# Block-sparse attention and a gated feed-forward layer on one core: another opening, and the last output tile in column halves

## The chip, the cores and the metric

The kernel runs on one core of a Trainium2 chip. The metric is the device time of one execution in microseconds (us). The five engines work from queues of their own: TensorE (PE: matmuls and transposes), VectorE (DVE), ScalarE (ACT), GpSimd (POOL) and SyncE (SP); SP, ACT and POOL also issue DMA transfers. An engine takes its instructions strictly in the order in which they were written for it; an instruction that waits for a semaphore holds all behind it. All times below are us.

## The reference

q, k and v have the shape (4 batches, 8 heads, 768 rows, 64). The rows form 24 blocks of 32. A query block sees its own key block and its two neighbours, the first and the last block, and three sampled blocks; the first and last query block see all. The result goes through RMS normalization and a gated feed-forward layer of width 1536.

```python
scores = scale * np.matmul(q, k.transpose(0, 1, 3, 2))
mask = np.abs(blk_i - blk_j) <= window          # window = 1
mask = mask | (blk_i == 0) | (blk_j == 0) | (blk_i == n_blocks - 1) | (blk_j == n_blocks - 1)
for qb in range(n_blocks):
    for kb in sampled_blocks[qb]:
        mask[qb * block:(qb + 1) * block, kb * block:(kb + 1) * block] = True
scores = np.where(mask, scores, -1000000000.0)
# softmax over the keys, then attn @ v; heads side by side give x of (3072, 512)
xn = x / np.sqrt(np.mean(x * x, axis=-1, keepdims=True) + 1e-06) * rms_g
out = (silu(xn @ w_gate) * (xn @ w_val)) @ w_out
```

## The kernel before

**Tiling.** The 3072 rows are worked through in 12 chunks of 256 query rows, three a batch. A chunk's attention has 12 tiles: 4 pairs of heads, and for each pair 3 pairs of 128-row key tiles. For a tile PE makes the scores (`scores`, L605: four products into a PSUM tile of two banks), ACT their exponential over 1024 columns (`exp_`, L624), DVE multiplies by a 0/1 mask tile (`mask_`, L631), and PE multiplies with V (`av`, L638). In chunk 0 there is no mask multiply. There PE adds a large negative number to the masked scores with a second product per score product (L619; `PEM`, L210, says for which chunks: chunk 0, and chunk 1 for the first `PM1` pairs, and PM1 is 0). So exponentials of chunk 0 can start before the mask tiles exist.

When a chunk's attention is done, DVE normalizes (`o_norm`), the squares are summed (`square`), POOL takes the power (`rstd`), DVE scales (`scale_x`), and the 256 x 512 result is transposed: on PE (`x_transposes`, L693, with a copy out of PSUM, `x_copy`), or for the chunks of `XDMA` (L721) by DMA transposes from SP's queue (`x_dma`). Then the feed-forward part follows: for each of 6 pairs of 128-column slices the gate product gp and the value product vp on PE (L839), tanh on ACT (L845), two DVE products (`ff_uu`, `ff_h`), and at last y, 12 products of 512 columns for each half chunk (`ff_y`, L862), which `ff_o` (L870) copies to SBUF and stores.

**Loads.** Two plain fp32 loads stand at the start: all of K of the first pair of heads (`kf`, L226, 384 KB, SP's queue) and the first two of the six column groups of Q of that pair (`qf`, L227, 128 KB, ACT's queue), and ACT casts them to bf16 (`cast_first`). The sampled blocks (`samp_i`, L232) follow on SP. POOL then issues loads that cast to bf16 on the way: Q of the other three pairs (q28), K of pair 1 (k23), K of pairs 2 and 3 (k48), then V in two halves, the rest of Q (qrest, needed from chunk 1 on), and the weights in halves (wg, wv) and whole (wo). Batches 1 to 3 are loaded as fp32 into one buffer in turn (K, then Q, then V; L258), cast by ACT or DVE in six steps (`cast_c`), and transposed by DMA.

**Mask.** tid holds, for block b and column, the column's distance from the start of block b. Two DVE instructions make the 0/1 indicator `Kind` from it (L317 and L319: distance at least 0, and at most 31). `block_mask` makes a 24 x 24 block matrix `Bm` from three small index tiles (`jb`, which POOL makes after its first load, L367 to L369), and `block_samples` (L343) adds the samples: one cast, three compare-and-max steps, one copy into a second half. PE multiplies R (two identities) with Kind (`key_rows`, L487) and Bm with Kind (`mask_query`, L497), copies bring both to SBUF as `KindG` and `NegQ`, and from these two PE makes the penalty in chunk 0 and the mask tiles `Mk` later (`mask_tile`, `mask_copy`).

**Order.** All steps except the first instructions are tasks of a planner (class `Plan`). It keeps a clock for each engine, estimates start and end of each task from a duration, the ends of its dependencies (a name with `>` ahead only orders; others wait for the result), free buffers (`acq`, `rel`), an estimated landing of each DMA (`dma`, `extra`) and an earliest time (`after`). It always emits the task with the smallest estimated start, plus `SOFT` times its priority (`PRIO` by class, with a `BOOST` for some). So the order of the instructions in every engine's queue is fixed before the run, by estimates. Score tiles have a gate: tile i is held back while i is more than `LEAD` tiles, plus `SPEED` times the share of feed-forward work that is done, ahead. Warm-up matmuls on zeros stand at PE's start (7, L302), and up to 40 fill gaps till 32 us in the planner's clock.

Of the kernel before, what the change touches and what calls it, by code (L numbers as in the profile page):

```python
# [8 lines left out]
FP32 = mybir.dt.float32  # L9
# [6 lines left out]
START = dict(DVE=3.4, POOL=1.7, ACT=2.5, PE=4.4)  # L16
DMA0 = 3.0
HOLD = 191057930523.28
SOFT = 0.0032
LEAD = 34  # L20
BOOST = {'first': 0.1, 'x': 0.15, 'w': -0.2}
SPEED = 0.91
PRIO = {'av': -5, 'c': 38, 'dt': 17, 'e': -23, 'g': -12, 'h': 1, 'm': 39, 'mk': 31, 'mq': -46, 'mqc': 32, 'mt': -5, 'on': 0, 'rs': 113, 's': -8, 'sc': 61, 'sq': -45, 't': 9, 'th': -85, 'uu': -15, 'v': -5, 'va': 6, 'x': -1, 'xc': -3, 'xd': -22, 'xt': 29, 'y': 2, 'yo': 5}
# [133 lines left out]
def kernel(  # L157
# [60 lines left out]
    QAT = (4.6, 20.0, 31.0)  # L218
# [5 lines left out]
    kf = raw.tile([P, 2, NC * D], FP32, name="kf")  # L224
    qf = raw.tile([P, 2, 2 * D], FP32, name="qf")
    nc.sync.dma_start(out=kf, in_=kv[0, :, 0:2, :])  # L226
    nc.scalar.dma_start(out=qf, in_=qv[0, :, 0:2, 0:2 * D])  # L227
# [4 lines left out]
    nc.sync.dma_start(out=samp_i[0:NB, :], in_=s64)  # L232

# [37 lines left out]

    tid = const.tile([32, S], I32, name="tid")
# [8 lines left out]
    jb = const.tile([32, 2 * 32 + 1], I32, name="jb")  # L281
    nhalf = const.tile([P, 2], FP32, name="nhalf")
    nc.vector.memset(nhalf, -0.5)
    ones = const.tile([P, 2], FP32, name="ones")
    nc.vector.memset(ones[:, 0:1], 1.0)
    nc.vector.memset(ones[:, 1:2], -16384.0)
    Bm = const.tile([32, P], BF16, name="Bm")
# [15 lines left out]
    for i in range(FILL):  # L303
# [12 lines left out]
    tif = const.tile([32, S], BF16, name="tif")  # L316
    nc.vector.tensor_scalar(  # L317
        out=tif, in0=tid, scalar1=0.0, scalar2=None, op0=ALU.is_ge)
    nc.vector.scalar_tensor_tensor(  # L319
        out=Kindf, in0=tid, scalar=31.5, in1=tif, op0=ALU.is_le, op1=ALU.mult)  # L320
    for lo in (0, 64):
        nc.vector.tensor_copy(out=R[:, lo:lo + 32], in_=ident[0:32, 0:32])
# [3 lines left out]
    samp_f = const.tile([32, NRND], FP32, name="samp_f")  # L326

    def block_mask():
# [7 lines left out]
            op0=ALU.is_equal, op1=ALU.max)  # L336
        nc.vector.tensor_scalar(
            out=Bm[:, 0:NB], in0=near[:, 0:NB], scalar1=1.0, scalar2=edge[:, 1:2],
            op0=ALU.is_le, op1=ALU.max)
        nc.vector.memset(Bm[:, 0:1], 1.0)  # L340
        nc.vector.memset(Bm[:, NB - 1:NB], 1.0)

    def block_samples():  # L343
        nc.vector.tensor_copy(out=samp_f[0:NB, :], in_=samp_i[0:NB, 0:2 * NRND:2])
# [622 lines left out]
```

## Time and profile before

| | us |
|---|---|
| median of 8 runs | 306.73 |
| lowest and highest | 304.64, 308.43 |
| the profiled execution, whole | 308.42 |
| its span, first to last instruction | 306.4 |
| PE busy | 293.5 |
| DVE busy | 246.8 |
| ACT busy | 220.0 |
| POOL busy | 33.5 |
| DMA: bytes over the span | 35.37 MB, mean 115 GB/s |

The profile is one execution. A row of it gives start, length, engine, source line, operation, output and inputs, and in brackets how long the engine was idle before and what released it. In rows of a window, the busy times of the engines follow the window's length. The chain of waits is the chain of work that ended last, followed back from the end. A group's row of DMA transfers gives the time from issue to landing. The profiled execution is close to the highest of the runs.

### The profile page before, as it was taken

What the parts mean: (1) busy time and instruction counts of PE and PEld (TensorE: products, weight loads), DVE (VectorE), ACT (ScalarE), POOL (GpSimd) and SP (SyncE); (2) the same over time, 40 slices, a digit from 0 to 9 for tenths busy, and PEclk for the clock granted to TensorE, in tenths of its full rate; (3) what the DMA queues carried; (4) which work ended last, traced back from release to release, by engine and by line L of the source; (5) the groups of instructions that cost most, each with busy time, mean ns of one, the idle gap of its engine ahead of it and who ended that gap; (6) DMA issues with size and microseconds to landing.
All of it is one profiled execution on the core that took longest, in us unless ns stands there. A gap on an engine that the chain in (4) does not pass through costs nothing.

```text
span 306.4 us, 8007 instructions
## 1 busy us (share of the span) xinstructions
PE 293.5 (96%) x3377; PEld 209.1 (68%) x3404; DVE 246.8 (81%) x491; ACT 220.0 (72%) x311; POOL 33.5 (11%) x53
## 2 busy tenths in 40 slices
PE   8998999999999999879999999999999999999995
PEld 2675777685776777647677857866857857859582
DVE  6349999985798999588988999997977959948370
ACT  4699989455789788649879979887776778664231
POOL 9410000102002002020002011210000000000000
PEclk9999999999999999979999999999999999999999
DMA  7999981847900729979304293943002003000101
GB/s 124 288 210 210 208 268 33 202 158 201 201 3 2 242 58 168 137 126 239 51 19 156 89 237 141 175 137 103 4 30 76 2 2 105 0 36 34 36 34 68
DMA packets 38839, 35.37 MB, mean 115 GB/s; under 512 B 26068, under 2 KB 32212, under 8 KB 38804
## 3 DMA queue, kind: packets, MB, share of 16 engines
q0 software_dynamic: 10128, 21.76, 30.3%
q1 hardware_dynamic: 28260, 12.85, 19.2%
q8 instruction: 26, 0.43, 0.6%
q10 hardware_dynamic: 416, 0.26, 0.3%
q14 instruction: 9, 0.07, 0.1%
HBM read 28.57 MB, written 6.29 MB: 114 GB/s over the span
## 4 chain that ended last, share of the span: by engine, by line
PE 79%; DMA 8%; DVE 5%; issue 3%; ACT 3%; POOL 0%; SPq 0%; ACTq 0%; DVEq 0%
PE yp L866 18%; PE vp L839 16%; PE gp L839 15%; PE gv L839 5%; DMA stage<-in_q_dram 4%; DMA stage<-in_v_dram 3%; ACT pt L628 2%; DVE uu L849 1%; DVE hp L856 1%; PE tq L439 1%; DMA samp_i<-in_sampled_blocks_dram 1%; PE xT L698 1%; PE of L649 1%; POOL stage L258 0%; DVE qb L252 0%
## 5 line engine op out<-in xcount | busy, mean ns | idle before, releaser
L635 DVE TENSOR_TENSOR pt<-pt,Mk 128x1024 bf16<-128x1024 bf16 x132 | 87.2, 684 | 8.1 <-ACT pt L628 7.9
L839 PE MATMUL vp<-xn,wv 128*128 128x256 bf16 x512 | 70.5, 275 | 3.5 <-DVE uu L849 3.0
L866 PE MATMUL yp<-wo,hp 128*128 128x512 bf16 x264 | 68.8, 382 | 1.2 <-issue 0.2
L839 PE MATMUL gp<-xn,wg 128*128 128x256 bf16 x512 | 66.4, 273 | 0.2 <-DVE hp L856 0.2
L839 PEld LDWEIGHTS <-wg 128*128 128x128 bf16 x576 | 55.6, 98 | 10.8 <-issue 1.9
L839 PEld LDWEIGHTS <-wv 128*128 128x128 bf16 x576 | 52.0, 98 | 12.3 <-issue 6.8
L649 PEld LDWEIGHTS <-pt 128*128 128x128 bf16 x1152 | 45.9, 97 | 15.8 <-issue 6.3
L845 ACT ACTIVATE th<-gp 128x512 bf16<-128x512 f32 x64 | 38.4, 600 | 22.7 <-PE gp L839 21.4
L849 DVE SCALAR_TENSOR_TENSOR uu<-th,gp 128x512 bf16<-128x512 bf16 x64 | 43.6, 681 | 5.4 <-ACT th L845 4.9
L856 DVE TENSOR_TENSOR hp<-uu,vp 128x512 bf16<-128x512 bf16 x64 | 43.4, 680 | 1.2
L866 PEld LDWEIGHTS <-hp 128*128 128x128 bf16 x288 | 25.4, 98 | 23.9 <-issue 3.0
L613 PEld LDWEIGHTS <-qkT 64*128 64x128 bf16 x576 | 23.7, 95 | 19.7 <-issue 16.5
L883 ACT ACTIVATE yo<-yp 128x512 f32<-128x512 f32 x23 | 13.7, 598 | 23.4 <-PE yp L866 23.2
L682 POOL TENSOR_TENSOR rs<-ms,nhalf 128x2 f32<-128x2 f32 x12 | 9.2, 763 | 172.2 <-ACT junk L674 124.3
L687 DVE SCALAR_TENSOR_TENSOR x<-X,rs,gB 128x512 bf16<-128x512 f32 x24 | 17.3, 746 | 6.1 <-POOL rs L682 5.9
L674 ACT ACTIVATE junk<-X 128x513 bf16<-128x513 f32 x20 | 12.5, 633 | 2.5 <-DVE X L663 2.5
L849 DVE SCALAR_TENSOR_TENSOR uu<-th,gv 128x512 bf16<-128x512 bf16 x8 | 5.5, 686 | 7.7 <-ACT th L845 7.5
L845 ACT ACTIVATE th<-gv 128x512 bf16<-128x512 f32 x8 | 4.8, 598 | 6.7 <-PE gv L839 6.7
L258 POOL DMA_DIRECT2D stage<-in_v_dram x8 | 6.1, 772 | 25.7 <-DVE qb L252 13.6
L258 POOL DMA_DIRECT2D stage<-in_q_dram x6 | 4.5, 757 | 36.5 <-ACT th L845 36.5
L839 PE MATMUL gv<-xn,wg 128*128 128x256 bf16 x64 | 8.5, 273 | 0.0
L445 DVE COPY qkT<-tq 128x256 bf16<-128x256 bf16 (+2 forms) x9 | 3.6, 421 | 5.9 <-PE tq L439 5.7
(521 smaller groups left out, 416.1 us busy)
## 6 DMA issues: line engine op xcount, KB each, us to landing
stage<-in_v_dram POOLq DMA_DIRECT2D x8, 768.0 KB, 9.3
out_dram<-yo SPq DMA_DIRECT2D x23, 256.0 KB, 2.3
stage<-in_k_dram POOLq DMA_DIRECT2D x6, 768.0 KB, 6.5
stage<-in_q_dram POOLq DMA_DIRECT2D x6, 768.0 KB, 8.0
wg<-in_moe_w_gate_dram POOLq DMA_DIRECT2D x2, 768.0 KB, 19.2
wv<-in_moe_w_val_dram POOLq DMA_DIRECT2D x2, 768.0 KB, 22.5
wo<-in_moe_w_out_dram POOLq DMA_DIRECT2D x1, 1536.0 KB, 30.9
qb<-in_q_dram POOLq DMA_DIRECT2D x1, 512.0 KB, 13.1
```

Of the source, the lines that this page charges most:

```text
L258: nc.gpsimd.dma_start(out=stages[b, i][:, lo:hi, :], in_=(qv, kv, vv)[i][b, :, lo:hi, :])
L613: nc.tensor.matmul(out=s_[:, e, jj * CQ:(jj + 1) * CQ], lhsT=x[rows, 1, 2 * j2 + jj, pr, :], rhs=x[rows, 0, 2 * ic:2 * ic + 2, pr, :], sta ...
L635: nc.vector.tensor_tensor(out=pv, in0=pv, in1=m.unsqueeze(1).to_broadcast([P, 2, 2 * CQ]), op=ALU.mult)
L649: nc.tensor.matmul(out=o_[:, qt, e, 0:D + 1], lhsT=pt[:, j2, e, jj * CQ + qt * P:jj * CQ + (qt + 1) * P], rhs=va[(ch // NIC) % 2][:, 2 * p ...
L674: nc.scalar.activation(out=junk, in_=x, func=AF.Square, scale=float(DM) ** -0.5, accum_out=ms)
L687: nc.vector.scalar_tensor_tensor(out=x2s[ch, qt], in0=x1s[ch][:, qt, 0:DM], scalar=mss[ch][:, qt:qt + 1], in1=gB, op0=ALU.mult, op1=ALU.mult)
L839: nc.tensor.matmul(out=pp[:, half * CQ:(half + 1) * CQ], lhsT=w[:, c, f * P:(f + 1) * P], rhs=xns[u][:, c, :], start=(c == 0), stop=(c == ...
L845: nc.scalar.activation(out=ths[u, fp], in_=gst[u, fp, "gp"], func=AF.Tanh, scale=0.5)
L849: nc.vector.scalar_tensor_tensor(out=uus[u, fp], in0=ths.pop((u, fp)), scalar=1.0, in1=gst.pop((u, fp, "gp")), op0=ALU.add, op1=ALU.mult)
L856: nc.vector.tensor_tensor(out=hps[u][:, 2 * fp:2 * fp + 2, :].rearrange("p f t -> p (f t)"), in0=uus.pop((u, fp)), in1=gst.pop((u, fp, "vp ...
L866: nc.tensor.matmul(out=yst[u, t], lhsT=hps[u][:, f, t * P:(t + 1) * P], rhs=wo[:, f, :], start=(f == 0), stop=(f == NF - 1))
L883: nc.scalar.activation(out=yo, in_=yp, func=AF.Copy, scale=0.5)
```

## The change

- **Loads.** K of pair 0 is loaded in two pieces (columns 0 to 127 first, then the rest), Q of pair 0 as before, and now K of pair 1 and the first two column groups of Q of pair 1 come by plain fp32 loads too, on SP's queue behind the samples. The casting loads that POOL issues become q48 (Q of pairs 2 and 3), k45 (K of pair 2), k67 (K of pair 3). Six casts, each on ACT or DVE, replace three. The index tiles `jb` are made ahead of `tid` and of the first POOL load.
- **Mask chain.** `Kind` comes from one ACT square of (tid - 15.5) and one DVE compare with 248. `block_mask` writes both halves of Bm at once. `block_samples` is one compare over 24 x 24 x 3, one max-reduction, one max into Bm. The two key products go into one score buffer (`s`) instead of two `f` banks, and the first query product into the `o` bank.
- **Order of the opening.** K transposes of pair 0 come ahead of its Q transposes; the K transposes of pair p are placed behind score tile 2p - 2 (counted from 0). The first score tiles wait for the first half of KindG only.
- **Transposes of x.** Chunks 2 and 5 leave `XDMA` and are transposed on PE.
- **Last y.** The last half chunk is made as two runs of 12 products of 256 columns. The first is copied by ACT and stored by SP; of the second, ACT and DVE copy 128 columns each, into tiles of their own, and ACT and SP store them.
- **Planner.** START, HOLD, SOFT, LEAD, BOOST, SPEED, PRIO and the landing estimates (`extra`) have other values.

`PEM`, `PM1`, the warm-up matmuls, the feed-forward loops up to y and the loads of batches 1 to 3 stay as they are.

```diff
-LEAD = 34
+LEAD = 82
-SPEED = 0.91
+SPEED = 1.02
...
-    kf = raw.tile([P, 2, NC * D], FP32, name="kf")
-    qf = raw.tile([P, 2, 2 * D], FP32, name="qf")
-    nc.sync.dma_start(out=kf, in_=kv[0, :, 0:2, :])
-    nc.scalar.dma_start(out=qf, in_=qv[0, :, 0:2, 0:2 * D])
+    kf = [raw.tile([P, 2, w * D], FP32, name=f"kf{w}") for w in (2, NC - 2, NC)]
+    qf = [raw.tile([P, 2, 2 * D], FP32, name=f"qf{i}") for i in range(2)]
+    nc.sync.dma_start(out=kf[0], in_=kv[0, :, 0:2, 0:2 * D])
+    nc.scalar.dma_start(out=qf[0], in_=qv[0, :, 0:2, 0:2 * D])
...
     nc.sync.dma_start(out=samp_i[0:NB, :], in_=s64)
+    nc.sync.dma_start(out=kf[1], in_=kv[0, :, 0:2, 2 * D:])
+    nc.sync.dma_start(out=kf[2], in_=kv[0, :, 2:4, :])
+    nc.sync.dma_start(out=qf[1], in_=qv[0, :, 2:4, 0:2 * D])
...
-    nc.vector.tensor_scalar(
-        out=tif, in0=tid, scalar1=0.0, scalar2=None, op0=ALU.is_ge)
-    nc.vector.scalar_tensor_tensor(
-        out=Kindf, in0=tid, scalar=31.5, in1=tif, op0=ALU.is_le, op1=ALU.mult)
+        nc.scalar.activation(
+            out=tsq, in_=tid, func=AF.Square, scale=1.0, bias=ones[0:32, 2:3])
+        nc.vector.tensor_scalar(
+            out=Kindf, in0=tsq, scalar1=248.0, scalar2=None, op0=ALU.is_le)
...
     def block_samples():
-        nc.vector.tensor_copy(out=samp_f[0:NB, :], in_=samp_i[0:NB, 0:2 * NRND:2])
-        for r in range(NRND):
-            nc.vector.scalar_tensor_tensor(
-                out=Bm[0:NB, 0:NB], in0=jbf[0:NB, 0:NB], scalar=samp_f[0:NB, r:r + 1],
-                in1=Bm[0:NB, 0:NB], op0=ALU.is_equal, op1=ALU.max)
-        nc.vector.tensor_copy(out=Bm[0:NB, 64:64 + NB], in_=Bm[0:NB, 0:NB])
+        nc.vector.tensor_tensor(
+            out=hit[0:NB], in0=jbf[0:NB, 0:NB].unsqueeze(2).to_broadcast([NB, NB, NRND]),
+            in1=samp_i[0:NB, 0:2 * NRND:2].unsqueeze(1).to_broadcast([NB, NB, NRND]),
+            op=ALU.is_equal)
+        nc.vector.tensor_reduce(
+            out=near[0:NB, 0:NB], in_=hit[0:NB], op=ALU.max, axis=mybir.AxisListType.X)
+        Bm2 = Bm.rearrange("b (r j) -> b r j", r=2)
+        nc.vector.tensor_tensor(
+            out=Bm2[0:NB, :, 0:NB], in0=Bm2[0:NB, :, 0:NB],
+            in1=near[0:NB, 0:NB].unsqueeze(1).to_broadcast([NB, 2, NB]), op=ALU.max)
...
-    swdge("q28", lambda: load_q(2, 8, 0, 2), 2.0, prio=-9, issue=1.05, extra=0.75)
-    swdge("k23", lambda: load_k(2, 4), 1.1, [">jb"], -9, extra=0.75)
-    swdge("k48", lambda: load_k(4, 8), 2.9, [">k23"], -9, extra=0.75)
-    swdge("V0", lambda: load_v0(0), 3.1, [">k48", ">sta0"], -9, extra=0.75)
+    swdge("q48", lambda: load_q(4, 8, 0, 2), 1.4, prio=-9, issue=1.0, extra=1.3)
+    swdge("k45", lambda: load_k(4, 6), 1.45, [">q48"], -9, extra=1.6)
+    swdge("k67", lambda: load_k(6, 8), 1.45, [">k45"], -9, extra=2.0)
+    swdge("V0", lambda: load_v0(0), 3.1, [">k67", ">sta0"], -9, extra=1.8)
...
-                 deps=["qrest"] if c0 and not i else LOADED[i, pr] + (
-                     [">" + before] if before else []))
+                 deps=["qrest"] if c0 and not i else FIRST[pr, i, c0] + (
+                     [">" + before] if before else []) + (
+                     [f">s{2 * pr - 2}"] if pr and i and not c0 else []))
...
-    XDMA = (2, 5, 8, 9, 10)
+    XDMA = (8, 9, 10)
...
-        if (u, t) == (NCH - 1, 1):
-            lo, hi = slice(0, DM // 2), slice(DM // 2, DM)
-            nc.scalar.activation(out=yo[:, lo], in_=yp[:, lo], func=AF.Copy, scale=0.5)
-            nc.vector.tensor_scalar(
-                out=yo[:, hi], in0=yp[:, hi], scalar1=0.5, scalar2=None, op0=ALU.mult)
-            nc.scalar.dma_start(out=dst[:, lo], in_=yo[:, lo])
-            nc.sync.dma_start(out=dst[:, hi], in_=yo[:, hi])
+        if half == 1:
+            for k, (lo, hi) in enumerate(((0, DM // 4), (DM // 4, DM // 2))):
+                yo = ffw.tile([P, DM], FP32, name="yo", tag="yo")[:, 0:DM // 4]
+                if k:
+                    nc.vector.tensor_scalar(
+                        out=yo, in0=yp[:, lo:hi], scalar1=0.5, scalar2=None, op0=ALU.mult)
+                else:
+                    nc.scalar.activation(out=yo, in_=yp[:, lo:hi], func=AF.Copy, scale=0.5)
+                (nc.sync if k else nc.scalar).dma_start(
+                    out=dst[:, DM // 2 + lo:DM // 2 + hi], in_=yo)
```

## The prediction, made before the changed kernel was run

> **What bounds the kernel now.** I read the page's busy shares and slices first.
>
> ```profile
> PE 293.5 (96%) x3377; PEld 209.1 (68%) x3404; DVE 246.8 (81%) x491; ACT 220.0 (72%) x311; POOL 33.5 (11%) x53
> ...
> PE   8998999999999999879999999999999999999995
> ```
>
> PE is the bound almost everywhere; slices under 9 are the opening, the end, and 122 to 138 us. So work removed from ACT or DVE is worth nothing by itself. PE's time falls only by less PE work, or by the feed-forward products starting sooner. The windows show where that can be:
>
> ```profile
> 10.00:20.00 10.00, 9.11 (x152) 6.55 (x150) 4.73 (x11) 8.33 (x10) 2.83 (x4) 1.00 1.18 281
> 20.00:30.00 10.00, 8.91 (x148) 6.26 (x146) 8.22 (x21) 9.09 (x12) 0.72 (x1) 1.00 1.16 210
> 30.00:40.00 10.00, 10.00 (x149) 7.33 (x148) 9.93 (x20) 9.57 (x13) 0.00 (x0) 1.00 1.22 210
> ...
> 130.00:132.00 2.00, 0.00 (x0) 0.00 (x0) 1.23 (x3) 1.24 (x3) 0.00 (x0) 1.00 0.32 112
> 132.00:134.00 2.00, 1.82 (x9) 1.31 (x9) 2.00 (x6) 1.70 (x2) 0.00 (x0) 0.54 0.67 127
> ```
>
> Columns: window, length, busy of PE, weight load, DVE, ACT, POOL, then granted clock, DMA share, GB/s. From 30 on everything is full. Before that PE is busy, but with attention that waits on ACT, and with idle fillers. The chain of waits of the first 60 us (start, length, what) gives the order:
>
> ```profile
> 1.26 3.35 DMA samp_i<-in_sampled_blocks_dram
> ...
> 5.62 0.52 DVE Bm L349
> ...
> 6.18 0.39 PE qm L500
> ...
> 11.60 0.47 issue
> ...
> 29.29 0.87 PE gp L839 x8
> ```
>
> The sampled blocks land at 4.61, five DVE instructions finish the block mask at 6.13, its product follows, and the first feed-forward product comes at 29.12 in the timeline (29.29 here). Between, ACT's exponentials of chunk 0:
>
> ```profile
> 8.83 1.02 ACT L628 ACTIVATE pt<-s__211 128x1024 bf16<-128x1024 f32 x1 [0.60 <-PE s__211 L619]
> ...
> 11.65 1.02 ACT L628 ACTIVATE pt<-s__255 128x1024 bf16<-128x1024 f32 x1 [0.88 <-PE s__255 L619]
> ...
> 13.46 1.02 ACT L628 ACTIVATE pt<-s__284 128x1024 bf16<-128x1024 f32 x1 [0.79 <-PE s__284 L619]
> ...
> 20.71 1.10 ACT L628 ACTIVATE pt<-s__443 128x1024 bf16<-128x1024 f32 x1
> ...
> 24.73 1.05 ACT L628 ACTIVATE pt<-s__551 128x1024 bf16<-128x1024 f32 x1
> ```
>
> Number 1 starts at 8.83, number 12 ends at 21.81, with two holes of 0.88 and 0.79. Elsewhere they follow each other every 0.905. After the last one, normalizing and transposing chunk 0 take 7.3 until the first product. That product also needs weights (min/median/max from issue to landing; first the gate's, then the value's):
>
> ```profile
> DMA to landing us min/median/max: 16.0/19.2/22.4
> ...
> DMA to landing us min/median/max: 19.6/22.5/25.4
> ```
>
> Issues at 7.02, 7.77, 8.74 and 9.48 make landings of 23.0, 27.4, 31.1 and 34.9. First uses are at 29.12, 31.49 and (second halves) from about 40.5: the start can move by about 4 before a weight stops it.
>
> The hole at 130 is something else: DVE and ACT stood at the head of their queues with casts of a late Q load.
>
> ```profile
> 130.77 0.76 DVE L252 CAST qb<-stage 128x512 bf16<-128x512 f32 x2 [4.06 <-issue]
> ...
> 132.18 1.23 PE L839 MATMUL vp<-xn,wv 128*128 128x256 bf16 x5 [2.75 <-DVE uu L849]
> ```
>
> It costs 2.75 of idle PE, and 2 x 0.46 + 2 x 0.39 = 1.70 in the 4 us after it at clocks of 0.54 and 0.61: 4.5 in all. The profiled execution took 308.42 (span 306.4, 2.0 around it), 1.7 above the median of 306.73; the fastest took 304.64. So I read this hole as part of the spread, mostly present in slow executions.
>
> **The change, part by part.**
>
> *Shorter mask chain.* The five DVE instructions take 1.50 (4.63 to 6.13). Three replace them, of 72, 72 and 48 elements a partition. The nearest row is 0.18 for 32 fp32 elements, so about 0.25 each: 0.75 (0.54 if 0.18 each, 1.50 if like the 0.51 copy). The samples now queue on SP behind 128 KB rather than 384: I take a landing of 4.0 (no better than 3.0, the 1.7 of a quiet 128 KB store after 1.26; no worse than 4.61). With two casts of some 0.3 between, the mask is ready near 5.2 instead of 6.13.
>
> The key indicator loses two DVE instructions (0.63 + 0.95) and gains an ACT square of 768 (0.83, the row of the 768-wide V cast) and one DVE compare (0.45; 0.25 to 0.63). The three small index instructions of POOL (0.35 together) move ahead of its large one, which ends near 2.0; the activation table loads until 2.53. So Kind is ready near 3.9 instead of 3.27. The seven warm-up matmuls hide that: PE is in them until 4.36. Without them it would cost 0.6.
>
> *First score.* In PE's order there now stand 8 transposes, two key matmuls, one query matmul and 8 more transposes. Spacings from the rows: 0.071 (four transposes in 0.43 with 0.217 each), 0.32, 0.21. 4.36 + 0.57 + 0.64 + 0.21 + 0.57 = 6.35, with the query copy (0.47) done at 6.43. First exponential 1.09 after that, as now: 7.5 instead of 8.83. Summing whole records instead gives 8.1. I take 7.6: gain 1.2.
>
> *The two holes.* The first (0.88) comes from 16 transposes of pair 1 (1.00) ahead of the third score tile; the second (0.79) contains PE's 0.47 wait for the load of K pairs 2 and 3. Now pair 1 arrives by plain loads, and each pair's K transposes stand behind an earlier score tile. Here a rule speaks against it: the Trainium skill, "DMA: Bandwidth & Descriptors", section "Issuing engines are not separate DMA queues", says that DMAs of all issuers interleave on the same 16 engines, so other issuers save only issue time. The transfer rate of the first 12 us in 40 slices:
>
> ```profile
> GB/s 0 0 0 0 0 0 87 157 232 333 396 369 161 57 19 50 97 140 157 166 198 191 126 81 95 108 110 125 141 154 172 243 212 287 311 416 343 382 396 345
> ```
>
> By the rule pair 1 would come no sooner than now (issue 3.13 + 5.2 = 8.3): holes as today, gain 1.2 only. By the row the engines ran dry from 3.9 to 4.8 (57, 19, 50): the 512 KB added to the plain loads fit there, at 350 to 390 GB/s in 1.4, landing near 5.4. I take the row for pair 1. For K of pair 2 I take the rule: the same bytes lie ahead, so it lands between 8.3 and 11.4 and its transposes, behind score tile 3, may hold PE and the scores behind them a little. Of the 1.67 I count 1.4 as gained (0 to 1.67).
>
> A second rule, "TensorE: Matmul & The Clock Gate", section "What's actually happening", says about 3.4 us of sustained work bring the full clock. The trace is slower: PE is nearly full from 1.19, but two score tiles still take 1.89 at 7.74 to 9.63, and 0.57 each only from 12.8, with the page's granted clock at 1.00 throughout. By the rule both holes would close and the first score would come 0.6 sooner (gain 3.5 instead of 2.6). I take the row.
>
> *V and rest of Q.* V's first issue moves from 4.61 to about 4.9, with equal bytes ahead; it lands near 14.9 as now. Number 12's AV product comes at about 20, so V is covered by some 3; the rest of Q (landing 19.2) by some 1. Chunk 0 thus ends 2.6 sooner, the first product comes at 26.5, the first value product at 28.9, against weights at 27.4: cover 1.5, after which each us late costs one. Opening: **-2.6** (-0.7 to -3.5).
>
> *Chunks 2 and 5 transposed on PE.* Two times 8 transposes of 0.056 spacing: **+0.9** on the bound engine (0 if they fall into a wait, 1.2 by whole records). The two added 0.68 copies lie under PE, DVE being at 9.2 of 10 at chunk 2; without that cover 0.7 each. Four DMA transposes leave SP's queue; the best that frees is the 0.5 of idle PE at 82 to 84, behind a V load. I take 0.
>
> *Last y.* The end now:
>
> ```profile
> 302.83 0.38 ACT L877 ACTIVATE yo<-yp 128x256 f32<-128x256 f32 x1 [1.99 <-PE yp L866]
> ...
> 303.24 0.42 DVE L878 TENSOR_SCALAR yo<-yp 128x256 f32<-128x256 f32 x1 [4.36 <-ACT yo L877]
> ```
>
> DVE waits for ACT, then copies 256 columns. After: 128 each in tiles of their own. The last tile is the fourth of a ring of three, so it waits for the store issued at 300.86 to land (+2.3 = 303.16): the DVE start hardly moves, the copy shrinks by 0.15, the store by 0.1 to 0.2. With 12 more hidden weight loads: **-0.3** (-0.7 to +0.2).
>
> *Chunk 1's mask on VectorE* changes nothing: 132 mask multiplies are 11 chunks of 12 already, only chunk 0 uses PE. *Order of everything else*: the planner's constants change, and with them each cast's place; LEAD 34 to 82 lets attention run further ahead. Bounds: -1.7 (the hole gone: profile against median) to +4.5 (a second hole). I take 0: the kernel has six such Q and K loads and shows one hole.
>
> Sum: -2.6 + 0.9 - 0.3 = -2.0. Profiled execution 308.4 to 306.4; median 306.73 to **304.7**.
>
> **Rivals.** (a) *The gain is gone before 30.* Pair 2's K or the weights hold PE in order, so only the mask's 1.2 or less comes through: -1.0 + 0.9 - 0.3 gives 306.3. For it: DMA is saturated from 5 to 43. Against: 4 us of room before the weights. (b) *The hole at 130 closes too*: 304.7 - 1.7 = 303.0; only the new order speaks for it. (c) *Slower: a second hole.* A Q or K load lands after the place where its casts stand in the DVE and ACT queues; tanh and the gate products queue behind them and PE starves. Place: a batch load between 55 and 195; price 4.5, by the one seen: 306.73 - 2.0 + 4.5 = 309.2. It decides once such waits exceed the 2.0 gained. For it: landings of 11 to 16 us after issue; against: five of six loads fit. (d) *The mask part of the title does nothing*: it is in the sum, at 0.
>
> **How the numbers follow.** A measurement of this kernel tells about 0.5% from no change: under 305.2 is faster, over 308.3 slower. Forecast 0.50, own range 303.4 to 306.0 (four fifths of it under 305.2); (b) 0.19, (a) 0.20, (c) 0.11. Faster: 0.40 of the forecast, 0.19 of (b) and 0.03 of (a), 0.62. Slower: 0.09 of (c), its rest being a shorter hole. Same: 0.10 + 0.17 + 0.02 = 0.29. Range 302.2 to 307.2: it takes in (a), most of (b), and leaves out (c) and the lowest 0.07.
>
> **What would show it.** First exponential near 7.6, number 12 ending near 19.2, first product near 26.5, no holes of 0.8 between exponentials; 16 more x transposes on PE; 132 mask multiplies still; the last copy starting near 303 minus the shift. It is wrong if the first product doesn't move by over 1.5, or if PE shows a new idle stretch over 2 behind a cast.

## The result, and the profile after

The changed kernel takes 301.59 us (median of 11 runs, 300.75 to 302.87) against 306.13 for the kernel before, run beside it (32 runs, 304.04 to 308.92): ratio 0.985, 95% interval 0.982 to 0.988. The direction was forecast; the gain of 4.5 is over twice the forecast 2.0, and the time lies below the forecast range of 302.2 to 307.2. In what follows medians are over all runs of a kernel, while ratios leave out the runs that took over 1.5% more than its fastest one. The profiled execution of the changed kernel took 302.84, close to the highest of its runs; its span is 300.5.

The changed kernel's page, busy shares and slices (then the slices of the granted clock):

```profile
PE 290.5 (97%) x3397; PEld 208.5 (69%) x3426; DVE 249.1 (83%) x492; ACT 220.2 (73%) x315; POOL 33.3 (11%) x53
...
PE   6999999999989999999999999999999999999995
...
PEclk9799999999999999999999999999999999999999
```

Before, the two slices between 122 and 138 were under 9. Here both are 9, so 90% or more. The windows say the same (length, busy of PE, weight load, DVE, ACT, POOL, granted clock, DMA share, GB/s):

```profile
10.00:20.00 10.00, 9.68 (x165) 6.48 (x162) 4.92 (x12) 9.09 (x11) 1.68 (x3) 0.93 1.19 269
20.00:30.00 10.00, 9.39 (x162) 6.21 (x159) 8.96 (x22) 8.69 (x13) 1.92 (x3) 1.00 1.16 209
30.00:40.00 10.00, 10.00 (x129) 7.29 (x125) 9.88 (x21) 8.29 (x11) 0.00 (x0) 1.00 1.22 222
130.00:132.00 2.00, 2.00 (x15) 1.21 (x14) 1.86 (x4) 0.83 (x3) 1.00 (x2) 1.00 0.97 185
132.00:134.00 2.00, 2.00 (x32) 1.85 (x30) 1.19 (x4) 1.07 (x3) 0.53 (x1) 1.00 0.92 139
```

At 130 to 134 PE is full, at full clock. The longest idle time of PE behind the opening is now 1.06, at 84, where ACT and DVE had waited with a V cast for its load. The opening, in the changed kernel's timelines of PE, then ACT (exponentials 1, 3, 4 and 12 of chunk 0, then one of chunk 1), with the first gate product in the chain of waits last:

```profile
6.62 0.41 PE L459 MATMUL tq<-ident,kb 128*64 128x128 bf16 x8 [1.33 <-DVE kb L256]
```

```profile
8.66 1.02 ACT L651 ACTIVATE pt<-s__207 128x1024 bf16<-128x1024 f32 x1 [0.51 <-PE s__207 L642]
...
11.49 1.02 ACT L651 ACTIVATE pt<-s__252 128x1024 bf16<-128x1024 f32 x1 [0.89 <-PE s__252 L642]
12.53 1.02 ACT L651 ACTIVATE pt<-s__279 128x1024 bf16<-128x1024 f32 x1
...
19.78 1.10 ACT L651 ACTIVATE pt<-s__432 128x1024 bf16<-128x1024 f32 x1
23.51 1.05 ACT L651 ACTIVATE pt<-s__548 128x1024 bf16<-128x1024 f32 x1
```

```profile
27.41 0.98 PE gp L862 x8
```

Number 1 starts at 8.66 (before 8.83), number 4 at 12.53 (13.46), number 12 ends at 20.88 (21.81). The hole ahead of number 3 is still there, the one ahead of number 4 is gone in this profile. The first product comes at 27.34 in the timeline (29.12). The last y, in its timeline:

```profile
297.25 0.28 ACT L909 ACTIVATE yo<-yp 128x128 f32<-128x128 f32 x1 [0.93 <-PE yp L894]
...
297.56 0.29 DVE L906 TENSOR_SCALAR yo<-yp 128x128 f32<-128x128 f32 x1 [4.28 <-ACT yo L909]
```

DVE still copies after ACT. So this one profile, set against the one before, gives 1.8 at the first product and 4.1 behind it, of the 5.9 between the two spans.

### The profile page after: what moved, and what is told of

It is laid out like the page before. It is cut to its first block, busy times and chain, and to the rows that moved or that the text cites. A ratio compares the mean times of both kernels' runs of the same rounds, so it can differ in the third digit from the quotient of the medians.

```text
span 300.5 us, 8045 instructions
## 1 busy us (share of the span) xinstructions
PE 290.5 (97%) x3397; PEld 208.5 (69%) x3426; DVE 249.1 (83%) x492; ACT 220.2 (73%) x315; POOL 33.3 (11%) x53
## 4 chain that ended last, share of the span: by engine, by line
PE 87%; DMA 6%; ACT 4%; issue 1%; DVE 1%; SPq 0%; POOL 0%; ACTq 0%
PE yp L894 18%; PE vp L862 18%; PE gp L862 17%; PE gv L862 5%; DMA stage<-in_v_dram 5%; ACT pt L651 2%; DMA kf<-in_k_dram 1%; PE xT L721 1%; PE tq L459 1%; PE of L672 1%; PE mp L536 1%; ACT qb L256 0%; PE o__846 L672 0%; PE o__363 L672 0%; ACT qkT L465 0%
## 5 line engine op out<-in xcount | busy, mean ns | idle before, releaser
L658 DVE TENSOR_TENSOR pt<-pt,Mk 128x1024 bf16<-128x1024 bf16 x132 | 85.9, 684 | 0.6 <-ACT pt L651 0.6
L894 PE MATMUL yp<-wo,hp 128*128 128x512 bf16 (+1 forms) x271 | 66.7, 369 | 1.2
L862 PEld LDWEIGHTS <-wg 128*128 128x128 bf16 x576 | 56.0, 98 | 10.9 <-issue 0.6
L672 PEld LDWEIGHTS <-pt 128*128 128x128 bf16 x1152 | 45.0, 97 | 17.3 <-issue 7.2
L894 PEld LDWEIGHTS <-hp 128*128 128x128 bf16 x300 | 26.4, 97 | 20.4 <-issue 1.5
L915 ACT ACTIVATE yo<-yp 128x512 f32<-128x512 f32 (+1 forms) x24 | 14.1, 588 | 18.3 <-PE yp L894 18.1
L697 ACT ACTIVATE junk<-X 128x513 bf16<-128x513 f32 x22 | 13.8, 630 | 2.7 <-DVE X L686 2.5
L256 DVE COPY xn<-xT 128x1024 bf16<-128x1024 bf16 (+1 forms) x11 | 6.5, 589 | 2.4 <-PE xT L721 2.4
L862 PE MATMUL gv<-xn,wv 128*128 128x256 bf16 x64 | 8.3, 273 | 0.0
```

Of the source, the lines that this page charges most:

```text
L658: nc.vector.tensor_tensor(out=pv, in0=pv, in1=m.unsqueeze(1).to_broadcast([P, 2, 2 * CQ]), op=ALU.mult)
L672: nc.tensor.matmul(out=o_[:, qt, e, 0:D + 1], lhsT=pt[:, j2, e, jj * CQ + qt * P:jj * CQ + (qt + 1) * P], rhs=va[(ch // NIC) % 2][:, 2 * p ...
L697: nc.scalar.activation(out=junk, in_=x, func=AF.Square, scale=float(DM) ** -0.5, accum_out=ms)
L862: nc.tensor.matmul(out=pp[:, half * CQ:(half + 1) * CQ], lhsT=w[:, c, f * P:(f + 1) * P], rhs=xns[u][:, c, :], start=(c == 0), stop=(c == ...
L894: nc.tensor.matmul(out=yst[u, t, half][:, 0:n], lhsT=hps[u][:, f, t * P:(t + 1) * P], rhs=wo[:, f, cols], start=(f == 0), stop=(f == NF - 1))
L915: nc.scalar.activation(out=yo, in_=yp[:, 0:n], func=AF.Copy, scale=0.5)
```

## The experiments

In all but one of them (a_old_y) the kernel's own order of tasks was written out as a list and followed, so that only the named edit differs. Names with b_ start from the kernel before, names with a_ from the changed one. Ratios are to runs of the kernel before on the same chip. "Landing" is from issue to landing of the two halves of batch 2's Q load, as minimum, median and maximum.

### Is it where the casts stand?

b_casts_later moves the six casts of batch 2's Q some 4 later in the queues of DVE and ACT; a_casts_early moves them 4 earlier in the changed kernel.

```diff
 # order of tasks
-... c2_0_0 ... c2_0_5 (the plan's 124 to 127)
+... c2_0_0 ... c2_0_5 (the plan's 128 to 131)
```

> The kernel before in its own order, with one difference: the six casts of batch 2's Q, and what depends on them, stand about 4 us (in the planner's clock) later in the DVE and ACT queues. Theory A (the hole at 130 is a cast at the head of both queues, and it is on average half there): PE's idle time of 2.7 at 129 to 132 and the half clock after it are gone, the time falls by 1.5 to 2.5 to about 304, and the runs spread less than 304 to 309. Rival B (the load itself is late and PE starves for it wherever the casts stand): the hole moves a few us later, the time stays within 0.5 of 306.1. Rival C (the gain of the change is all opening, the hole is a chance of one profile): no change of time.

> The changed kernel in its own order, with the six casts of batch 2's Q about 4 us (in the planner's clock) earlier in the DVE and ACT queues. Theory A: the hole comes back, 1 to 3 of idle PE near 125 to 129 with a half clock after it, the time rises by 1.5 to 4 to 303 to 305.5, and the spread widens. Rival B: the load lands late whatever the place, and the changed kernel does not wait for it now because it lands sooner; then the casts find their data and nothing changes (301.6). Rival C: no change.

b_casts_later: 306.08, ratio 0.999 (0.995 to 1.003). The casts no longer wait, but the hole has moved on: V uses the same buffer and is loaded when Q's casts are done, and now V's cast waits (and PE for it, 1.60 at 143.8), in the timeline of b_casts_later:

```profile
144.80 0.56 DVE L256 CAST va<-stage 128x768 bf16<-128x768 f32 x1 [2.67 <-DMA stage<-in_v_dram]
```

a_casts_early: 301.41, ratio 0.985 (0.982 to 0.989): no hole, although the first cast starts only 10.6 behind the issue of the load; before, DVE stood ready for it 12.1 behind and still had to wait. So the casts' place is not it. The load itself lands sooner, in 6.8 and 8.2 here, and the experiments below are about that.

### What the opening gives

a_mq_first puts the mask's query product and the first score tile ahead of the eight transposes of K's second piece:

```diff
 # order of tasks
-... t0_1_2 e0_1_2 ... mq0 ... s0
+... mq0 ... s0 t0_1_2 e0_1_2
```

b_k_split issues K of pairs 2 and 3 as two loads in the kernel before:

```diff
-    swdge("k48", lambda: load_k(4, 8), 2.9, [">k23"], -9, extra=0.75)
+    swdge("k48", lambda: (load_k(4, 6), load_k(6, 8)), 2.9, [">k23"], -9, extra=0.75)
```

> The changed kernel in its own order, but the query product of the mask and the first score tile stand ahead of the eight transposes of the rest of K of pair 0 in PE's queue, and the copy of those transposes follows. Theory A (the first score was late because PE stood 1.3 for the cast of a late piece of K, with the ready mask product behind it): first exponential at 7.5 to 7.8 instead of 8.66, the last of chunk 0 ends 0.4 to 0.9 sooner, the time falls by as much, to about 301.0. Rival (the third score tile, behind pair 1's transposes at the slow PE rate, sets the pace): first exponential sooner, third unmoved near 11.5, time unmoved.

> The kernel before in its own order, with the casting load of K of pairs 2 and 3 issued as two loads, so that pair 2's transposes wait for pair 2's K only. Theory F (this landing, 11.4 to 12.3, sets the opening of the kernel before, whichever clock PE has till then): the fourth exponential starts at 12.3 to 13.0 instead of 13.5 to 14.2, PE's wait at 10 to 12 falls from 2.5 to 1.5 or less, the first feed-forward product comes at 28 to 29.5 instead of 29.1 to 31.1, the time falls by 0.7 to 1.5. Rival (V, issued 0.8 later, or ACT's rate sets the rest): fourth exponential sooner, first product and time unmoved.

a_mq_first: the first exponential starts at 7.00, 1.66 sooner, but the third only at 10.88 and the fourth at 12.63; 301.63, ratio 0.986 (0.983 to 0.990), no gain over the changed kernel. (In its profile the granted clock is 0.5 from 8 to 14, so its starts can't be compared to the tenth.) The start of the first exponential is not what the opening is worth.

b_k_split: 304.98, ratio 0.997 (0.993 to 1.000), a gain that is just not clear of noise. In its profile the fourth exponential starts at 10.91, the first product at 26.58, and PE no longer waits for K. How much it had waited shows in b_casts_later, where PE came there earlier than in the profile that the prediction used (0.47):

```profile
11.89 0.85 PE L443 MATMUL tq<-ident,kb 128*64 128x128 bf16 x12 [2.46 <-DMA kb<-in_k_dram]
```

With K in one load this is the end of the wait in either case, 11.9 or 12.1. An earlier first product can thus be had by one more DMA instruction; what it is worth in time is seen better without the hole, further down.

### The x transposes on PE, and the last y

b_x_on_pe takes chunks 2 and 5 out of `XDMA` in the kernel before; b_sl_x_on_pe does it in a version without the hole (b_split_late, below); a_x_by_dma puts them back on DMA in the changed kernel, each as soon as its rows are scaled. a_old_y gives the changed kernel the old last y.

```diff
-    XDMA = (2, 5, 8, 9, 10)
+    XDMA = (8, 9, 10)
 # order of tasks
-... sc2_0 xd2_0 sc2_1 xd2_1 ... (and chunk 5)
+... sc2_0 sc2_1 ... xt2 xc2 ... (and chunk 5)
```

```diff
     # a_old_y: the last half chunk as in the kernel before
-        return (u, t) == (NCH - 1, 1)
+        return False
...
+            nc.scalar.dma_start(out=dst[:, lo], in_=yo[:, lo])
+            nc.sync.dma_start(out=dst[:, hi], in_=yo[:, hi])
```

> The kernel before in its own order, with chunks 2 and 5 transposed on PE instead of by DMA, at the place in the queues that follows their scaling. Prediction's step: 16 transposes on the bound engine cost 0.9, so 307.0. Rival (four DMA transposes fewer on SP's queue let batch 1's Q transposes and V load land sooner): no cost or a gain, 305 to 306.

> The kernel before in its own order with K of pairs 2 and 3 in two loads, batch 2's Q load 0.76 later, and chunks 2 and 5 transposed on PE. Without the x edit this took 301.54 and had no hole. Theory (16 transposes of 0.056 on PE, nothing else): +0.9, 302.2 to 302.8. Rival (the 1.9 seen with the hole still there holds here too, since copies on a full DVE delay the mask products): 303.2 to 304.2.

> The changed kernel in its own order, with chunks 2 and 5 transposed by DMA from SP's queue again, each issued as soon as its rows are scaled. If 16 transposes on PE cost their 0.9 and the DMA transposes are hidden: 300.2 to 301.0, faster than the changed kernel. Rival: some 3 of other work lies between the scaling and the first gate product of the chunk, and the DMA transposes take about as long, so PE waits for x at chunk 2 or 5 (0.5 to 2 each) and the time is 301.5 to 304; or the four transposes on SP's queue meet a load and bring a hole back.

> The changed kernel with the end of the kernel before: one run of 12 products of 512 columns for the last half chunk, copied in two halves of 256 columns by ACT and DVE. The prediction put the column halves at -0.3 (-0.7 to +0.2): 301.9. Rival (the serial copies and the small stores make no difference, or the 12 added weight loads cost as much): 301.5.

b_x_on_pe: 308.5, ratio 1.009 (1.005 to 1.012). b_sl_x_on_pe: 305.25, 0.998 (0.995 to 1.001), where b_split_late has 0.985 (0.982 to 0.987): 0.0135 of 306, so 4.1. That is over both expectations. In the groups of PE, of b_split_late and then of b_sl_x_on_pe, the transposes add 1.2:

```profile
L707 PE MATMUL xT<-ident,x 128*128 128x128 bf16 x56 | 4.6, 219 | 0.4 <-DVE xn L256 0.4
```

```profile
L848 PE MATMUL vp<-xn,wv 128*128 128x256 bf16 x512 | 69.7, 272 | 1.5 <-ACT yo L892 1.3 <-DVE uu L858 0.2
...
L707 PE MATMUL xT<-ident,x 128*128 128x128 bf16 x72 | 5.8, 219 | 0.4 <-DVE xn L256 0.4
```

The 1.3 in the second fence (busy us, mean ns, then idle before and its releaser) is new: ACT is late for PE because it stood with a cast of batch 1's V, which lands up to 11.1 after its issue instead of 8.6: with the x transposes gone from SP's queue, Q's last two transposes are issued sooner, 1.3 ahead of the V load and beside it instead of 1.1 and 2.5 behind. These two make 2.5 of the 3.2 between the two profiles; the rest of the 4.1 is not accounted for.

a_x_by_dma: 313.3, ratio 1.022 (1.016 to 1.027). In the changed order the two DMA transposes of chunk 2 are issued 4.6 and 6.2 behind a V load and take 8.8 and 7.7 to land, where the kernel before shows 2.5 for one that was issued 1.9 ahead of that load. PE waits, in a_x_by_dma's timeline:

```profile
69.14 1.49 POOL L266 DMA_DIRECT2D stage<-in_v_dram  x2 [15.07 <-ACT qb L260]
...
73.73 4.05 SPq L743 DMA_TRANSPOSE xn<-x  x2
...
83.10 1.89 PE L866 MATMUL gp<-xn,wg 128*128 128x256 bf16 x8 [7.65 <-DMA xn<-x]
```

It waits 2.52 more at chunk 5, and behind the first wait the granted clock is 0.50 from 84 to 88. So the price of these 16 transposes depends on the order around them: a loss of 2.7 to 4.1 in one order, a saving of some 11 in the other (0.037 of 306, from 1.022 and 0.985), against DMA transposes at this place in the queue.

a_old_y: 301.12, ratio 0.985 (0.980 to 0.990), as the changed kernel. The last y makes no difference that these runs can tell.

### When is batch 2's Q load late?

The load waits for the last K cast; so does the second of the two K transposes. In the kernel before SP stands until 112.35 with the store of chunk 2's second half, whose y is late in the order, and so issues the first transpose only at 112.79, some 1.2 later than without that store (b_store_behind below: 3.05 ahead of the load instead of 1.86). The trace of the kernel before, DMA issues, and the landing of the load:

```profile
100.07 12.62 SPq L884 DMA_DIRECT2D out_dram<-yo  x2
...
112.79 3.28 SPq L475 DMA_TRANSPOSE qkT<-kb  x2
114.65 1.49 POOL L258 DMA_DIRECT2D stage<-in_q_dram  x2 [14.86 <-ACT th L845]
...
DMA to landing us min/median/max: 11.4/13.3/15.3
```

In the changed kernel that y is in SBUF some 8 ahead of the transposes:

```profile
98.26 5.62 SPq L916 DMA_DIRECT2D out_dram<-yo  x2
...
111.36 3.29 SPq L495 DMA_TRANSPOSE qkT<-kb  x2
...
113.50 1.49 POOL L262 DMA_DIRECT2D stage<-in_q_dram  x2 [13.44 <-DVE uu L872]
...
DMA to landing us min/median/max: 7.4/8.1/8.7
```

Five experiments move only these issues: in b_load_late, b_small_delay and b_mid_delay POOL copies 512, 128 and 256 columns ahead of the load (added work), in b_store_behind the store is issued behind the two transposes, in a_transpose_late SP makes two small copies within SBUF ahead of the second transpose. The first diff is b_load_late (the others with 128 or 256 columns), the second a_transpose_late, the third b_store_behind.

```diff
     def load_part(b, i, lo, hi):
+        if (b, i, lo) == (2, 0, 0):
+            nc.gpsimd.tensor_copy(
+                out=pj, in_=kraw[b].rearrange("p h w -> p (h w)")[:, (NC - 1) * DM:NC * DM])
```

```diff
     def transposes_dma(b, i, c0, c1):
+        if (b, i, c0) == (2, 1, 3):
+            for n in range(2):
+                nc.sync.dma_start(
+                    out=pj[:, n * 64:(n + 1) * 64],
+                    in_=kraw[b].rearrange("p h w -> p (h w)")[:, (NC - 1) * DM + n * 64:(NC - 1) * DM + (n + 1) * 64])
```

```diff
     def transposes_dma(b, i, c0, c1):
...
+        if (b, i, c0) == (2, 1, 3):
+            nc.sync.dma_start(out=held[0][0], in_=held[0][1])
...
     def ff_o(u, t):
...
+        if (u, t) == (2, 1):
+            held.append((dst, yo))
+            return
         nc.sync.dma_start(out=dst, in_=yo)
```

> The kernel before in its own order; ahead of batch 2's Q load, POOL copies the 512 columns that the last K cast wrote, so the load is issued 0.4 to 1.5 later and stands clearly behind the second K transpose of that batch. (The copy is added work; nothing is left out.) Theory D (whether the load is issued before or after the start of the second K transpose decides how the two share the DMA engines): the load takes 6.5 to 9 instead of 11.4 to 15.3, the Q casts no longer wait at 126 to 131, the idle of 100 to 160 falls from 3 to under 1, the time falls by 2 to 4 to 302.5 to 304.5. Rival E (the load is slow for another reason, such as its place in SBUF or the time of day in the run): it stays at 11 to 15, the hole moves with it by 0.4 to 1.5, and the time is the same or a little longer, 306 to 307.5.

> The changed kernel in its own order; ahead of batch 2's second K transpose SP issues two small copies from SBUF to SBUF that wait for the same cast, so the transpose is issued about 0.8 later, behind the Q load instead of 0.27 ahead of it. (Added work; nothing is left out.) Theory D: the Q load takes 11 or more instead of 6.7 to 9.1, its casts wait and PE shows a hole near 128: 303 to 305.5. Rival E: the load stays under 10, the time stays within 0.7 of 301.5.

> The kernel before in its own order, POOL copies only 128 columns ahead of batch 2's Q load: the load is then issued some 0.2 to 0.4 behind the last K transpose (with 512 columns it was 0.76, without the copy 0.02). Theory (only issues at the same moment collide; the changed kernel has 0.27 and is fast): the load lands in 6 to 9.5, no hole, 302.5 to 304. Rival (it takes most of a microsecond, so that the transpose's own transfers are done; the changed kernel is fast for another reason): landing 10 or more, a hole of over 1.5, time 305.5 to 307.

> The kernel before in its own order, POOL copies 256 columns ahead of batch 2's Q load; 128 columns (first transpose 2.05 ahead) left it slow at 12.9 to 14.1, 512 (2.33 ahead) made it fast at 7.3 to 8.6. Here the first transpose is about 2.15 ahead. Theory (the limit lies near 2.1): fast, landing under 10, 302.5 to 304. Rival (it takes the 0.7 behind the second transpose): slow, landing over 11, 305 to 306.5.

> The kernel before in its own order; only the store of the second half of chunk 2's y is issued by SP behind batch 2's two K transposes instead of ahead of them (the K transposes then are not held by it). Theory (a store ahead of transposes and load is what makes them crawl): the load lands in 9.5 or less, no idle stretch over 1.5 between 110 and 150, time 302.3 to 304. Rival (the store has nothing to do with it; load and transpose at the same moment, in this order): landing 11 to 15, hole of over 2, 305 to 307.5.

| run | first transpose ahead of the load | landing | us | ratio (interval) |
|---|---|---|---|---|
| kernel before | 1.86 | 11.4/13.3/15.3 | 306.1 | 1 |
| b_small_delay | 2.01 | 12.9/13.5/14.1 | 305.46 | 0.996 (0.993 to 0.998) |
| b_mid_delay | 2.12 | 7.8/8.5/9.1 | 302.46 | 0.989 (0.986 to 0.992) |
| b_load_late | 2.33 | 7.3/8.0/8.6 | 303.15 | 0.990 (0.985 to 0.995) |
| b_store_behind | 3.05 | 7.4/8.4/9.4 | 302.43 | 0.988 (0.986 to 0.991) |
| changed kernel | 2.14 | 7.4/8.1/8.7 | 301.59 | 0.985 (0.982 to 0.988) |
| a_transpose_late | 2.13, second 1.02 behind | 5.4/6.2/7.1 | 301.1 | 0.985 (0.980 to 0.990) |

One tenth of a us between b_small_delay and b_mid_delay decides. (That b_small_delay, with the hole, is 0.4% below the kernel before is not explained.) Their landings and windows, first b_small_delay, then b_mid_delay:

```profile
DMA to landing us min/median/max: 12.9/13.5/14.1
...
125.00:130.00 5.00, 3.28 (x45) 2.65 (x44) 1.96 (x6) 3.33 (x5) 0.00 (x0) 1.00 0.41 146
130.00:135.00 5.00, 4.58 (x36) 2.51 (x36) 4.96 (x11) 1.73 (x3) 1.53 (x2) 1.00 1.05 166
```

```profile
DMA to landing us min/median/max: 7.8/8.5/9.1
...
125.00:130.00 5.00, 5.00 (x57) 3.77 (x56) 5.00 (x11) 4.55 (x7) 1.01 (x2) 1.00 0.69 155
130.00:135.00 5.00, 5.00 (x66) 3.48 (x64) 3.92 (x10) 2.85 (x5) 0.52 (x1) 1.00 1.03 138
```

And what the DMA engines do from 112 to 130, again b_small_delay and then b_mid_delay (GB/s in 40 slices; then the load's queue: packets, MB, share of 16 engines):

```profile
GB/s 255 209 210 217 175 179 151 170 176 161 162 24 89 88 71 69 122 129 166 154 190 1 21 108 98 154 327 346 440 294 373 294 158 151 139 96 9 0 0 0
...
q0 software_dynamic: 384, 1.57, 51.1%
```

```profile
GB/s 369 212 217 210 214 170 208 140 158 181 108 10 9 269 278 312 339 441 342 314 328 328 406 239 27 0 0 0 36 296 250 5 9 23 167 214 188 165 209 191
...
q0 software_dynamic: 384, 1.57, 26.0%
```

The same 384 packets hold the engines twice as long (51.1% against 26.0% of 16 engines x 18 us: 0.38 against 0.20 each), and for some 6.5 the transfers crawl at 1 to 190 GB/s instead of 270 to 440. The three edits of the kernel before that have no hole gain 3.0 to 3.4 by the medians, so this hole was in the median of the kernel before, and no matter of single executions. The traces agree: PE's idle time from 100 to 160 is 1.8 to 3.3 in the five profiles of the old order with the first transpose at most 2.01 ahead, and 0 to 0.5 in the six with it further ahead. One of the five, b_k_split's, is of one of that kernel's two quickest runs (303.38; the lowest is 303.35).

Three more ask why. a_coincide puts one small copy ahead of the second transpose in the changed kernel, a_store_ahead holds the store back to just ahead of the transposes, a_first_later delays the first transpose by a copy of 16 partitions that waits for the third K cast. (a_store_ahead keeps the store back as b_store_behind does.)

```diff
     def transposes_dma(b, i, c0, c1):
...
+        # a_coincide
+        if (b, i, c0) == (2, 1, 3):
+            nc.sync.dma_start(
+                out=pj[:, 0:64],
+                in_=kraw[b].rearrange("p h w -> p (h w)")[:, (NC - 1) * DM:(NC - 1) * DM + 64])
...
+        # a_first_later; a_store_ahead with all partitions, and the last line
+        if (b, i, c0) == (2, 1, 0):
+            nc.sync.dma_start(
+                out=pj[0:16], in_=kraw[b].rearrange("p h w -> p (h w)")[0:16, 3 * DM - 64:3 * DM])
+            nc.sync.dma_start(out=held[0][0], in_=held[0][1])
```

> The changed kernel in its own order, with one small copy within SBUF on SP ahead of the last K transpose of batch 2, so that this transpose and the Q load are issued within about 0.3 of each other. Theory (issue at the same moment is what makes the load slow): the load lands in 9.5 or more, its casts wait, PE shows an idle stretch of over 1 between 110 and 150, time 302.5 to 305. Rival (something else in the order of the kernel before makes it slow): landing 6 to 9, no hole, 300.5 to 302.

> The changed kernel in its own order; the store of the second half of chunk 2's y, issued 9 ahead of batch 2's K transposes, is held back in SP's queue (behind one small copy within SBUF that waits for the third K cast) until just ahead of them. Theory (the store is what matters): landing of 10 or more for batch 2's Q load, a hole of over 1 in PE between 115 and 150, 303 to 306. Rival (the store is harmless): landing 6 to 9.5, no hole, 301 to 302.3.

> The changed kernel in its own order, with one copy of 16 partitions within SBUF on SP, waiting for the third K cast, ahead of batch 2's K transposes: the first of them is issued some 0.2 to 0.5 later, so 1.6 to 1.95 ahead of the Q load, with the second still ahead of it by up to 0.3. Theory (both transposes within about 2.05 ahead of the load is what makes it slow, in any order): landing 10 or more, PE idle over 1 between 110 and 150, 302.5 to 305. Rival (only the order of before is slow, for a reason that the issue times do not show): landing 7 to 9.5, no hole, 301 to 302.

a_coincide: the second transpose is 0.4 behind the load; landing 6.0/7.6/9.3, 301.62, ratio 0.986 (0.982 to 0.989). a_store_ahead: first transpose 0.9 ahead, second 0.7 behind; landing 7.5/8.3/9.1, 302.2, 0.987 (0.985 to 0.990). Both expectations of a late load fell: neither issue at one moment nor the store alone makes it. a_first_later came out between: first transpose 1.45 ahead, the second 0.1 behind instead of ahead, landing 9.3/10.1/10.9, no hole, 301.39, 0.986 (0.983 to 0.990). What fits all traces: the load is late when both transposes are issued ahead of it, the first at most 2.01 ahead (all five kernels in the order of before where that holds), and not when the first is 2.12 or more ahead, or when the second comes behind the load. The Q loads of batches 1 and 3 fit too, in every trace: there the first stands 2.26 or more ahead, or the second behind, and they land in 6.4 to 10.3. In the changed order the case "both ahead, at most 2.01" was not reached, so that the line holds there too is not shown. What in the chip draws it stays open.

### The two causes together

b_split_late joins b_k_split and b_load_late, b_split_store joins b_k_split and b_store_behind and adds no work; their diffs are the ones shown.

> The kernel before in its own order of instructions, with two edits: K of pairs 2 and 3 is issued as two loads, and POOL copies 512 columns just ahead of batch 2's Q load, so that the load is issued about 0.76 behind the last K transpose instead of together with it. Theory (the gain of the change is the opening's wait for K plus the hole behind batch 2's Q load): both waits are gone, the load lands in 9 or less, no idle stretch over 2 between 100 and 160, first product before 28, time 301.0 to 302.5, all of the change's gain with none of its masks, loads by SP or x transposes. Rival (the gain of the change needs its shorter opening and its order too): the load edit alone had 303.15, the split alone -1, so 302.5 to 303.5 at best, or the two don't add.

> The kernel before with two edits that add no work: K of pairs 2 and 3 in two loads, and the store of the second half of chunk 2's y behind batch 2's K transposes. If the store is the cause of the slow load: 300.8 to 302, as good as the changed kernel or better. If not: the hole stays and the time is 304.5 to 306.

b_split_late: 301.54, ratio 0.985 (0.982 to 0.987). b_split_store: 301.75, 0.986 (0.983 to 0.988). The kernel before with one load split and one store moved is as quick as the changed one, within what the runs tell. Against b_store_behind on the same chip (302.43) the split is worth 0.7 by the medians, with intervals that overlap.

## Why the prediction was wrong in size

- **"Order of everything else ... I take 0"**: this is the step that failed, with its reason, "I read this hole as part of the spread, mostly present in slow executions". The hole is in every profile of the old order that keeps the first transpose at most 2.01 ahead of the load, and edits that touch only that load, or the store ahead of its transposes, are worth 3.0 to 3.4. The prediction set a bound of -1.7, profile against median, on a wait whose 4.5 it had just added up. Of this 4.5 the half clock behind the wait, 1.70, is in only two of the five profiles (mean granted clock from 130 to 140: 0.83; in the other three 1.00), which fits a median gain below 4.5. Rival (b) named the right event and priced it from that bound. That the new order closes the hole is luck as far as the change goes: no part of it aims there. Its first transpose stands 2.14 ahead of the load, where in the old order 2.12 was still quick and 2.01 was not. That this spacing is what closes the hole in the new order is argued from there and not shown: no edit of the changed kernel brought the hole back.
- **Opening, -2.6**: right in sign, mis-sized. The start of the first product varies by execution: 28.2 to 31.1 in seven profiles of the old order with K of pairs 2 and 3 in one load (mean 29.1), 26.2 to 29.2 in eight of the changed one with its opening untouched (mean 28.2). So it is worth about 1.0 there, known to about 1 either way, and less than one execution differs from another. The prediction's own sign of being wrong, a first product that doesn't move by over 1.5, shows in these means, though not in the one profile (1.8). With K of pairs 2 and 3 in two loads the old order reaches a mean of 27.5 (four profiles, 26.6 to 28.0).
- **First score, 7.6**: the first exponential starts at 8.66. The mask is ready at 4.57, sooner than the 5.2 assumed (three instructions of 0.20 to 0.22, below the 0.25 each), but PE waits 1.33 for the second piece of pair 0's K, issued at 1.78 and landing at 5.86. Splitting a load made a wait that the sum had not listed; and a_mq_first shows that the first start is worth nothing by itself.
- **Pair 1 by plain loads, "landing near 5.4. I take the row"**: pair 1's K lands at 6.9 and its Q at 8.2, where the rule said 8.3. The Trainium skill, "DMA: Bandwidth & Descriptors", section "Issuing engines are not separate DMA queues", was the better guide: the dip in this transfer rate was not room for 512 KB more. The hole ahead of exponential 3 stayed, 0.89 to 1.34 in all nine profiles of the changed order. In the changed kernel's own profile PE is full with the first two score tiles until 9.48, so the landing is not what it waits for there; in a_first_later, with a quicker PE, it waits 1.25 for the casts of pair 1, and the hole is 1.11. The hole ahead of number 4 closed in the changed kernel's own profile, as counted, but in five of the other eight it is 0.61 to 0.73. In the old order K's landing is behind it, as b_k_split shows.
- **Clock, "I take the row"**: right for this execution. In the changed kernel's profile the granted clock is 0.7 in the second slice, though PE is at work from 1.19 on; and in profiles of both orders a score tile of the first 12 us takes 0.61 from its first product to its last in some executions and 1.04 in others. So part of the opening's spread is PE's rate in that execution and not the order. The granted clock does not always show it: in the profile of the kernel before it is 1.00 with tiles of 1.04.
- **x on PE, +0.9**: the work is +1.2 (whole records, the upper bound given), but the time +2.7 and +4.1 in the old order. "I take 0" for what leaves SP's queue was the weak half: in the old order it lets other transposes meet the V load sooner, and V lands later; in the changed order x by DMA, behind a V load, costs far more than x on PE. The step has no price of its own.
- **Last y, -0.3**: 0 within what the runs tell. **Mask on VectorE, nothing**: right, 132 multiplies as before. **Rival (c), a second hole**: did not come.

The traces of both orders put together: the first product comes about 1.0 sooner, and from there to the end the old order takes 274.9 to 277.3 in four profiles with the hole (without x on PE; mean 275.6), the changed one 271.7 to 273.1 in eight (all of its but a_x_by_dma; mean 272.1). -1.0 - 3.5 = -4.5, the measured gain; that it fits to the tenth is chance, given the spread. The old order without the hole (five profiles, x by DMA) takes 271.8 to 272.8 there, mean 272.3: so the closed hole makes nearly all of the 3.5, and all else that the new order does behind the opening comes to about 0 in sum. The forecast was -2.6 for the first part and +0.6 for the second.

## What to carry to other kernels

A wait seen in the one profile at hand belongs to the kernel until runs say otherwise; price it by what that profile shows (here 4.5, where the runs gave 3.0 to 3.4), and list as a rival of full weight that the change moves it. Look for what decides it in the issue queues: here a store that waited for a late y held two transposes on SP, and they were then issued close ahead of a load on POOL. Before building a new opening, split the one load that the engine waits for and move the one store: here two small edits gave what the whole change gave.

## What the runs showed of the hardware

A plain fp32 load of 1.5 MB in two halves, issued by POOL behind two DMA transposes, lands its second half in 7.7 to 10.3 or in 13.7 to 15.3, and a tenth of a us in the spacing of the issues (2.01 against 2.12) decides; its packets take 0.38 instead of 0.20 in the late case (b_small_delay against b_mid_delay). A pair of DMA transposes of x took 8.8 and 7.7, issued 4.6 and 6.2 behind such a load (a_x_by_dma), where most of the others took 2.4 to 2.6. Neither shows as busy time of a compute engine: only the landing times, the time of the DMA packets and the row of GB/s tell it.
